# Attention with head mixing and a token and channel mixer on one core: the sums' 1e-9, the places of weight conversion, the places of v and k loads

## The chip, the cores and the metric

The kernel runs on one core of a Trainium2 chip. The metric is the device time of one launch in microseconds (us); lower is better. The engines in the text are PE (TensorE; PEld is its weight load), DVE (VectorE), ACT (ScalarE), POOL (GpSimd) and SP (SyncE), which issues nearly all DMAs.

## What is computed

```python
scores = scale * (q @ k.T)                           # 4 batches, 12 heads, 448 x 448, head_dim 64
scores = einsum('bhij,hg->bgij', scores, w_pre)      # mix the 12 heads
scores = scores - max(scores, -1)
attn = exp(scores) / (sum(exp(scores), -1) + 1e-09)
attn = einsum('bhij,hg->bgij', attn, w_post)         # mix the heads again
x = concat_heads(attn @ v)                           # (4, 448, 768)
u = x + (relu(x.T @ w_tok1) @ w_tok2).T              # 448 -> 256 -> 448
out = u + relu(u @ w_ch1) @ w_ch2                    # 768 -> 1536 -> 768
```

Everything is float32; the weights of the last two lines arrive as 64-bit numbers and are converted on the chip.

## The kernel before, in words

**Attention, tiled.** Each batch's 448 query rows are cut into four tiles T of 120, 120, 120 and 88 rows, 16 tiles in all. For a tile, `qk` (L129) makes the scores of a pair of heads on PE and copies them to the tile `s` (ACT, L146). `regroup` (L156) takes ten query rows with their 12 heads each and moves them by DMA from `s` to one of eight tiles `r`, so that 120 partitions hold (head, row) pairs. On such a group `pre` (L161) mixes heads on PE, `mx` (L171) takes the negated row maximum on DVE into the small tile `sm`, `ex` (L177) does the exponential on ACT, whose accumulator writes the row sums to `sm`, and `rec` (L188) makes the reciprocals on DVE (an add of 1e-9 at L192, the reciprocal at L193) and lets POOL scale the tile `e` with them (L195 short, L198 long). `post` (L200) mixes heads again on PE, `turn` (L213) transposes on DVE (L220), and `av` (L224) multiplies by v on PE; ACT copies one half of its result to `x` (L249), DVE adds the other (L251), and a DMA stores it (L252). Two groups sit side by side on 128 partitions and are one entry of `steps`: 92 entries, one in 23 with a single group.

**The loop.** The main loop (L447) runs J from -2 to 45, two entries of `steps` per J, in an order written out by hand that every engine follows in its own queue. In step J, `pa` and `pb` are posted and turned (entries 2J and 2J+1), `ea` and `eb` get their exponentials and `rec` (2J+2, 2J+3), `na` and `nb` their `pre` and `mx` (2J+4, 2J+5), and entries 2J+8 and 2J+9 are regrouped; what is regrouped in step J is read by `pre` in step J+2. Between these stand one `av` (`value[J]`) and mostly two `qk` (`score[J]`; three in J = 5, 6, 8, 28, 29 and 31, one beside two `av` in 10 and 33, none from 40 on). PE's order in a step is post, post, pre, av, qk, pre, qk; DVE's is turn, rec, turn, rec, mx, add of av, mx.

**PSUM.** Post, av and qk results share two buffers of a pair of banks (`pair("w", ...)`), in turn: the second qk of a step can start only when DVE's add (L251) has emptied av's buffer. `pre` has two of its own.

**Loads.** `loads[J]` are issued at the head of step J on SP's queue, before the step's regroups: q by `uses[T] - 2`; v of batch b in four parts of 384 KB, two at a time (L439); k of batch b in three parts of two DMAs of 224 KB, one part per step (L442).

**Weight conversion.** `cv_tick` (L394) works on a pipeline over `units`. One tick at position i issues the load of unit i+5 (SP, L349), copies unit i's rounded half (ACT, L370), does three bit operations of unit i+1 (DVE, L379, L383, L389), subtracts for unit i's low half (POOL, L387), clamps for unit i+2 (POOL, L361) and takes magnitudes for unit i+3 (ACT, L355). Positions start at -5; units 0 to 3 are w_tok1, 4 to 7 are w_tok2, the rest channel weights. Ticks stand in the last four steps of the loop (L476), after the loop (L580), and in the token phase (two in each `tok1`, three in each `tok2` but the first).

**After the loop** the last tile's three `av` alternate with the PE transpositions `tr` of batch 0 (L499), then `tok1` and `tok2` run for four batches, with `tr` of the next batch between them, and then the channel phase, `ch1` and `ch2`.

Of the kernel before, what the change touches and what calls it, by code (L numbers as in the profile page):

```python
# [8 lines left out]
F32 = mybir.dt.float32  # L9
# [5 lines left out]
ALU = mybir.AluOpType  # L15
AX = mybir.AxisListType
# [9 lines left out]
HP = H // 2  # L26
NR = 8
NE = 4
KD = DM // 128
NC = DC // 128  # L30
WARM = 11
# [4 lines left out]
def attn_mixer_kernel(  # L36
# [12 lines left out]
    nc = tc.nc  # L49
# [24 lines left out]
    mid = en("mid", bufs=2)  # L74
# [5 lines left out]
    kpost = mid.tile([128, 64], F32, bufs=1, name="kpost")  # L80
    et = [mid.tile([128, 2, 512], F32, bufs=1, name=f"e{i}") for i in range(NE)]
    rt = [mid.tile([128, S], F32, bufs=1, name=f"r{i}") for i in range(NR)]
    AT, V = {}, {}

    K = {}
    Q = {}
    S_t, R, E, SM, PP, PO = {}, {}, {}, {}, {}, {}
    ne = [0]

    groups = []  # L90
    first = []
# [78 lines left out]

    def mx(st):  # L171
        m = 64 * len(st)
        s = mid.tile([128, 8], F32, tag="sm", bufs=6, name="sm")
        nc.vector.tensor_reduce(out=s[:m, 0:2], in_=PP[st[0]][:m, :, :S], axis=AX.X, op=ALU.max, negate=True)  # L174
        SM[st[0]] = s

    def ex(st, x):  # L177
        m = 64 * len(st)
        s, p = SM[st[0]], PP[st[0]]
        if x == 0:  # L180
            E[st[0]] = et[ne[0] % NE]
            ne[0] += 1
        nc.scalar.activation(  # L183
            out=E[st[0]][:m, x, :S], in_=p[:m, x, :S], func=ACTF.Exp, bias=s[:m, x:x + 1], scale=1.0,
            accum_out=s[:m, 2 + x:3 + x],
        )

    def rec(st):  # L188
        m = 64 * len(st)
        s, e = SM.pop(st[0]), E[st[0]]  # L190
        PP.pop(st[0])
        nc.vector.tensor_scalar_add(out=s[:m, 4:6], in0=s[:m, 2:4], scalar1=1e-9)  # L192
        nc.vector.reciprocal(out=s[:m, 6:8], in_=s[:m, 4:6])  # L193
        w = s[:m, 6:8].unsqueeze(2)
        nc.gpsimd.tensor_tensor(  # L195
            out=e[:m, :, S:], in0=e[:m, :, 384:S], in1=w.to_broadcast([m, 2, 512 - S]), op=ALU.mult,
        )
        nc.gpsimd.tensor_tensor(out=e[:m, :, :S], in0=e[:m, :, :S], in1=w.to_broadcast([m, 2, S]), op=ALU.mult)  # L198
# [25 lines left out]
    def av(T, hp):  # L224
        b, t = divmod(T, 4)
        i0, n = IT[t]
        w = 12 if t < 3 else 9
        at_ = AT[T].rearrange("p c (g x f) -> p g c x f", g=2, x=2)
        p = pair("w", "av")
        for u in range(2):  # L230
            for j in range(JT):
                for r in range(2) if j < 3 else (u,):
                    k = slice(64 * r, 64 * r + 64)
                    for s in range(2):
                        h = 2 * hp + s
                        f = 32 * j + 5 * h
                        nc.tensor.matmul(  # L237
                            out=p[64 * s:64 * s + 64, r, 10 * w * u:10 * w * (u + 1)], lhsT=V[b][k, 6 * u + h, j, :],
                            rhs=at_[k, u, :w, :, f:f + 5], start=j == 0, stop=j == (3 if r == u else 2),
                        )  # L240
        x = late.tile([128, 2, 120], F32, tag="x", bufs=4, name="x")
        m = n // GR * GR
        y = p[:, :, :20 * w].rearrange("p r (u y) -> p r u y", u=2)
        cols = [(x[:, :, :m].rearrange("p u (k c) -> p u c k", k=GR), slice(0, m), GR)]
        if m < n:
            cols.append((x[:, :, m:n].unsqueeze(2), slice(m + 1, n + 1), n - m))
        cols = [(o, [y[:, r, :, c].rearrange("p u (c k) -> p u c k", k=k) for r in range(2)]) for o, c, k in cols]
        for o, (y0, _) in cols:
            nc.scalar.copy(out=o, in_=y0)  # L249
        for o, (_, y1) in cols:  # L250
            nc.vector.tensor_tensor(out=o, in0=y1, in1=o, op=ALU.add)  # L251
        nc.sync.dma_start(out=x_dr[b][:, hp:hp + 4:3, i0:i0 + n], in_=x[:, :, :n])  # L252

    two = (nc.sync, nc.scalar)
    one = (nc.sync, nc.sync)
# [2 lines left out]
        load_k(0, part, two)  # L258
    for i in range(2):
        nc.gpsimd.memset(kcat[i], 0.0)  # L260
    nc.gpsimd.dma_start(out=kcat[0][4:124], in_=wcat)
    for s in range(2):
        nc.gpsimd.dma_start(out=kcat[1][64 * s:64 * s + 60], in_=wcat[60 * s:60 * s + 60])
# [6 lines left out]
    for i in range(WARM):  # L270
        p = pair("w", "pw")
# [3 lines left out]
    for x in range(2):  # L275
        ps_ = slice(64 * x, 64 * x + 64)
        nc.vector.tensor_tensor(
            out=kpre[ps_, :60].rearrange("p (i g) -> p i g", i=5),
            in0=kcat[0][ps_, :12].unsqueeze(1).to_broadcast([64, 5, H]),
# [4 lines left out]
    for s in range(2):  # L284
        ps_ = slice(64 * s, 64 * s + 64)
        for hf in range(2):
            nc.gpsimd.tensor_tensor(
                out=kpost[ps_, 32 * hf:32 * hf + 30].rearrange("p (g i) -> p g i", g=6),
                in0=kcat[1][ps_, 12 + 6 * hf:18 + 6 * hf].unsqueeze(2).to_broadcast([64, 6, 5]),
# [104 lines left out]
    def cv_tick(k, eng=nc.gpsimd):  # L394
        for _ in range(k):
            i = cv_pos[0]
            if i >= cv_lim[0]:
                return
            if i + 5 < len(units):
                cv_load(i + 5)  # L400
            cv_step(i, eng)
            if 0 <= i + 2 < len(units):
                cv_clamp(i + 2)
            if 0 <= i + 3 < len(units):
                cv_abs(i + 3)
            cv_pos[0] += 1

    NS = len(steps)
    ND = NS // 2
    sf = [next(i for i, st in enumerate(steps) if st[0] == f) for f in first[:-1]] + [NS]  # L410
    loads = {J: [] for J in range(-2, ND)}
    score = {J: [] for J in range(-2, ND)}
    value = {J: [] for J in range(-2, ND)}
    for T in range(NT - 1):
        J = sf[T + 1] // 2
# [8 lines left out]
    for T in range(2, NT):  # L424
        hi = (sf[T] - 8) // 2
        lo = max((sf[T - 1] - 9) // 2 + 1, hi - 2)
        for h in range(HP):
            J = min(range(lo, hi + 1), key=lambda J: (len(score[J]) + len(value[J]), J))
            score[J].append((T, h))
    uses = {}  # L430
# [5 lines left out]
        loads[max(-2, uses[T] - 2)].append((load_q, T, one))  # L436
    for b in range(B):
        for part in range(JT):
            loads[max(0, sf[4 * b + 1] // 2 - 6) + part // 2].append((load_v, b, part))  # L439
        if b:  # L440
            for part in range(3):
                loads[uses[4 * b] - 5 + part].append((load_k, b, part, one))  # L442

    def step(i):
        return steps[i] if 0 <= i < NS else []
# [1 line left out]
    for J in range(-2, ND):  # L447
        pa, pb, ea, eb, na, nb = [step(2 * J + i) for i in range(6)]
        if J == ND - 4:
            close("early")  # L450
            open_prep()
        if J == ND - 1:
            close("ps")
            a2 = en("a2", bufs=2, side="right")
            pst = en("pst", bufs=4, space=PSUM, side="right")
        for fn, *a in loads[J]:
            fn(*a)
        if J in (ND - 3, ND - 2):
            load_x(J - ND + 3)
        for st in (pa, pb):  # L460
            if st:
                post(st)
        if ea:
            ex(ea, 1)
        if pa:
            turn(pa)
        if ea:
            rec(ea)
            ex(eb, 0)
            ex(eb, 1)  # L470
        if pb:
            turn(pb)
        if eb:
            rec(eb)
        if J >= ND - 4:
            cv_tick((2, 2, 3, 3)[J - ND])  # L476
        if na:
            pre(na)
            mx(na)
        for a in value[J][:1]:  # L480
            av(*a)
        for a in score[J][:1]:
            qk(*a)
        if nb:
            pre(nb)
            ex(na, 0)
        for a in value[J][1:]:
            av(*a)
        for a in score[J][1:]:
            qk(*a)  # L490
        if nb:
            mx(nb)
        for st in (step(2 * J + 8), step(2 * J + 9)):
            for G in st:
                regroup(G)
# [3 lines left out]
    def tr(b, hfs=(0, 1)):  # L499
        x = XR[b]  # L500
        xn = XN.get(b) or [a2.tile([128, JT - i, DM], F32R, tag=f"xn{i}", bufs=1, name=f"xn{i}") for i in range(2)]
        for hf in hfs:
            for j in range(JT):
                p = pst.tile([128, 512], F32, tag="tr", name="tr")
                for d in range(3):
                    nc.tensor.transpose(
                        out=p[:, 128 * d:128 * d + 128], in_=x[hf][:, d, min(128 * j, 320):min(128 * j, 320) + 128],
                        identity=prep["ident"],
                    )
                cs = slice(384 * hf, 384 * hf + 384)  # L510
                nc.scalar.copy(out=xn[0][:, j, cs], in_=p[:, :384])
                lo_t, r = (xn[1][:, j, cs], 0) if j < 3 else (xn[0][:64, 3, cs], 64)
                nc.vector.tensor_tensor(out=lo_t, in0=p[r:, :384], in1=f32(xn[0])[r:, j, cs], op=ALU.subtract)
        XN[b] = xn
# [27 lines left out]
    def tok2(b):  # L542
        h1 = H1.pop(b)
        x = XR.pop(b)
        us = []
        for d in range(KD):
            p = psa.tile([128, 512], F32, tag="t", bufs=4, name="pt2")
# [26 lines left out]

    av(NT - 1, 0)
    tr(0, (0,))
    av(NT - 1, 1)
    tr(0, (1,))
    av(NT - 1, 2)
    cv_tick(3)  # L580
    close("mid", "late", "atp", "ps_w")
    psa = en("psa", bufs=2, space=PSUM)
    prep["w"] = en("wres", bufs=1)
# [101 lines left out]
```

## Time and profile before

| | |
|---|---|
| median of 3 runs | 835.23 us (834.58 to 839.51) |
| the profiled execution's own time | 835.09 us |
| its span, first to last instruction | 833.0 us |
| busy in the span | PE 768.2, PEld 579.8, DVE 509.6, ACT 335.7, POOL 307.0 us |
| attention loop / its end and the token phase / channel phase | to about 377 / to about 480 / to 833 us |

How to read the rows below: times are us from the span's start. A timeline row gives start, duration, engine, line, operation, output<-input tiles, sizes and count; the square bracket says how long the engine had been idle just before, and which instruction ended that idle time. PEclk is the granted TensorE clock as a share of full speed. In the chain of work that ended last, each row is a piece of the path, followed back from the last instruction. A PE matmul's end is modelled, so that matmuls which follow each other appear to overlap.

### The profile page before, as it was taken

The numbers are of one execution on the slowest core, as the hardware profiler recorded it, in microseconds if no ns is written. First come the engines' busy times: TensorE is split into PE (matmuls) and PEld (weight loads), VectorE is DVE, ScalarE is ACT, GpSimd is POOL, SyncE is SP. The second block draws the span as 40 slices with busy tenths as digits, with TensorE's granted clock in tenths as the row PEclk, the third lists the DMA queues.
The fourth block names the chain that finished last, engine by engine and source line by source line (L and its number), as shares of the span: only waits on it lengthen the run. The fifth ranks groups of instructions, "written<-read, shape, count | busy, mean of one in ns | idle before, by whom it ended". The sixth has DMA issues, their size and how long they took to land.

```text
span 833.0 us, 21918 instructions
## 1 busy us (share of the span) xinstructions
PE 768.2 (92%) x9211; PEld 579.8 (70%) x9211; DVE 509.6 (61%) x816; ACT 335.7 (40%) x757; POOL 307.0 (37%) x292
## 2 busy tenths in 40 slices
PE   7788888999888888886899999999999999999998
PEld 3344545455445454445688899999999999999997
DVE  4867788888887788898889989964000400030002
ACT  3646656666666656554454334432000200020000
POOL 3645454555554555576536857730000000000000
PEclk9989999999999999997999999999999999999999
DMA  6874646456644643365356755543000300010001
GB/s 169 246 203 119 181 160 206 154 130 232 191 159 131 201 148 126 123 195 179 104 171 227 225 173 172 171 170 134 1 1 1 133 1 1 1 67 1 0 1 67
DMA packets 62594, 105.66 MB, mean 127 GB/s; under 512 B 20979, under 2 KB 49184, under 8 KB 61984
## 3 DMA queue, kind: packets, MB, share of 16 engines
q1 hardware_dynamic: 62080, 103.35, 39.5%
q8 instruction: 73, 1.20, 0.6%
q10 hardware_dynamic: 320, 0.87, 0.4%
q14 instruction: 25, 0.20, 0.1%
q0 software_dynamic: 96, 0.03, 0.0%
HBM read 49.18 MB, written 16.52 MB: 79 GB/s over the span
## 4 chain that ended last, share of the span: by engine, by line
PE 72%; DVE 17%; issue 4%; DMA 3%; ACT 3%; POOL 1%; SPq 0%; DVEq 0%; POOLq 0%; ACTq 0%
PE post L207 7%; PE pc L522 7%; PE pc L521 7%; PE pc L523 7%; PE po L522 7%; PE po L521 7%; PE po L523 7%; PE qk L139 7%; DVE at L220 6%; PE av L237 5%; DVE sm L192 4%; PE pre L167 3%; DVE x L251 3%; PE pt L521 2%; PE pt L522 2%
## 5 line engine op out<-in xcount | busy, mean ns | idle before, releaser
L518 DVE SCALAR_TENSOR_TENSOR rl<-pc,rh 128x448 fp32r<-128x448 f32 x48 | 29.9, 622 | 224.8 <-ACT rh L517 224.8
L198 POOL TENSOR_TENSOR e<-e,sm 128x896 f32<-128x896 f32 (+1 forms) x92 | 154.6, 1680 | 7.2
L220 DVE STREAM_TRANSPOSE at<-post 128x1024 f32<-128x1024 f32 (+1 forms) x92 | 111.9, 1216 | 49.7 <-PE post L207 49.7
L517 ACT ACTIVATE rh<-pc 128x448 fp32r<-128x448 f32 x48 | 26.0, 541 | 242.8 <-PE pc L523 242.8
L183 ACT ACTIVATE e<-pre,sm 128x448 f32<-128x448 f32 (+1 forms) x184 | 114.9, 633 | 16.0 <-DVE sm L174 15.5
L207 PE MATMUL post<-e,kpost 64*32 64x256 f32 x2880 | 100.2, 382 | 22.7 <-DVE x L251 7.5
L139 PE MATMUL qk<-k,q 64*64 64x448 f32 (+2 forms) x768 | 94.7, 546 | 24.9 <-DVE x L251 23.4
L207 PEld LDWEIGHTS post<-e,kpost 64*32 64x32 f32 x2880 | 49.6, 106 | 82.4 <-POOL e L198 33.4
L523 PE MATMUL pc<-u,w 128*128 128x448 f32 x288 | 105.2, 365 | 0.0
L522 PE MATMUL po<-rl,w 128*128 128x448 f32 x288 | 105.2, 365 | 0.0
L522 PE MATMUL pc<-u,w 128*128 128x448 f32 x288 | 105.2, 365 | 0.0
L521 PE MATMUL po<-rh,w 128*128 128x448 f32 x288 | 105.2, 365 | 0.0
L521 PE MATMUL pc<-u,w 128*128 128x448 f32 x288 | 105.2, 365 | 0.0
L523 PE MATMUL po<-rh,w 128*128 128x448 f32 x288 | 105.2, 365 | 0.0
L174 DVE TENSOR_REDUCE sm<-pre 128x2 f32<-128x896 f32 (+1 forms) x92 | 99.6, 1085 | 7.0 <-PE pre L167 6.7
L167 PE MATMUL pre<-r,kpre 64*64 64x448 f32 (+1 forms) x720 | 96.5, 553 | 5.3 <-DMA r<-s 3.0
L195 POOL TENSOR_TENSOR e<-e,sm 128x128 f32<-128x128 f32 (+1 forms) x92 | 36.7, 399 | 169.1 <-DVE sm L193 145.4
L361 POOL TENSOR_SCALAR cv_g<-cv_g 128x384 f32<-128x384 f32 (+2 forms) x56 | 87.0, 1555 | 23.6 <-ACT cv_g L355 23.6
L237 PEld LDWEIGHTS av<-at,v 64*64 64x64 f32 x2688 | 79.2, 137 | 22.8 <-DVE sm L192 10.8
L146 ACT COPY s<-qk 120x896 f32<-120x896 f32 (+1 forms) x84 | 75.4, 905 | 36.7 <-PE qk L139 33.4
L237 PE MATMUL av<-at,v 64*64 64x120 f32 (+1 forms) x2688 | 84.5, 269 | 1.2 <-DVE x L251 1.0
L139 PEld LDWEIGHTS qk<-k,q 64*64 64x64 f32 (+2 forms) x768 | 29.6, 128 | 59.9 <-DVE x L251 33.6
(71 smaller groups left out, 1060.6 us busy)
## 6 DMA issues: line engine op xcount, KB each, us to landing
r<-s SPq DMA_DIRECT2D x176, 210.0 KB
cv_r<-in_w_ch_dram SPq DMA_DIRECT2D x48, 384.0 KB
v<-in_v_dram SPq DMA_DIRECT2D x16, 384.0 KB
xr<-x_dr SPq DMA_DIRECT2D x8, 672.0 KB
u_dr<-u SPq DMA_DIRECT2D x24, 224.0 KB
ur<-u_dr SPq DMA_DIRECT2D x4, 1344.0 KB
out_dram<-ur SPq DMA_DIRECT2D x24, 224.0 KB
k<-in_k_dram SPq DMA_DIRECT2D x21, 224.0 KB
```

What stands on the lines that cost most here:

```text
L139: nc.tensor.matmul(out=p[c:c + m, s, :S], lhsT=Q[T][r, h, c:c + m], rhs=K[b][r, h, :], start=True, stop=True)
L167: nc.tensor.matmul(out=p[64 * s:64 * s + 64, x, :S], lhsT=kpre[k], rhs=rt[a % NR][k], start=True, stop=True)
L174: nc.vector.tensor_reduce(out=s[:m, 0:2], in_=PP[st[0]][:m, :, :S], axis=AX.X, op=ALU.max, negate=True)
L183: nc.scalar.activation(out=E[st[0]][:m, x, :S], in_=p[:m, x, :S], func=ACTF.Exp, bias=s[:m, x:x + 1], scale=1.0, accum_out=s[:m, 2 + x:3 + x],
L198: nc.gpsimd.tensor_tensor(out=e[:m, :, :S], in0=e[:m, :, :S], in1=w.to_broadcast([m, 2, S]), op=ALU.mult)
L207: nc.tensor.matmul(out=p[32 * a:32 * a + 32, s, 256 * hf:256 * hf + 256], lhsT=kpost[k, 32 * hf:32 * hf + 32], rhs=ek[k, :, :, a, :], star ...
L220: nc.vector.transpose(out=AT[T][:, c:c + w].rearrange("p c f -> p (c f)"), in_=p[:, :w].rearrange("p c f -> p (c f)"))
L237: nc.tensor.matmul(out=p[64 * s:64 * s + 64, r, 10 * w * u:10 * w * (u + 1)], lhsT=V[b][k, 6 * u + h, j, :], rhs=at_[k, u, :w, :, f:f + 5] ...
L361: nc.gpsimd.tensor_scalar(out=g[:P], in0=g[:P], scalar1=MAG_MIN, scalar2=MAG_MAX, op0=ALU.max, op1=ALU.min,)
L521: nc.tensor.matmul(out=p, lhsT=a[0], rhs=x[0], start=first, stop=False)
L522: nc.tensor.matmul(out=p, lhsT=a[0], rhs=x[1], start=False, stop=False)
L523: nc.tensor.matmul(out=p, lhsT=a[1], rhs=x[0], start=False, stop=last)
```

## The change

The tile `sm`, so far drawn from a pool of six buffers of 8 columns, becomes six persistent tiles of 10 columns, filled with 1e-9 once at the start. ACT's accumulator writes the two row sums to columns 2 and 4, so that each has a 1e-9 beside it in columns 3 and 5. DVE's add of a constant (L192) becomes a sum over pairs of columns. Conversion ticks in the last four steps go from 2, 2, 3, 3 to 2, 1, 1, 3; after the loop one comes behind each of the two `tr`, and three become two at the end. Parts of v are loaded in four steps, one each, the last one step before the first use; k's three parts are loaded two in one step and one in the next, nearer to the first use.

```diff
+NM = 6
+    smt = [mid.tile([128, 10], F32, bufs=1, name=f"sm{i}") for i in range(NM)]
     def mx(st):
-        s = mid.tile([128, 8], F32, tag="sm", bufs=6, name="sm")
+        s = smt[ns[0] % NM]
+        ns[0] += 1
     def ex(st, x):
-            accum_out=s[:m, 2 + x:3 + x],
+            accum_out=s[:m, 2 + 2 * x:3 + 2 * x],
     def rec(st):
-        nc.vector.tensor_scalar_add(out=s[:m, 4:6], in0=s[:m, 2:4], scalar1=1e-9)
-        nc.vector.reciprocal(out=s[:m, 6:8], in_=s[:m, 4:6])
+        nc.vector.tensor_reduce(
+            out=s[:m, 8:10], in_=s[:m, 2:6].rearrange("p (x y) -> p x y", y=2), axis=AX.X, op=ALU.add
+        )
+        nc.vector.reciprocal(out=s[:m, 6:8], in_=s[:m, 8:10])
@@ start
+    for m in smt:
+        nc.vector.memset(m, 1e-9)
@@ loads
-            loads[max(0, sf[4 * b + 1] // 2 - 6) + part // 2].append((load_v, b, part))
+            loads[sf[4 * b + 1] // 2 - 4 + part].append((load_v, b, part))
-                loads[uses[4 * b] - 5 + part].append((load_k, b, part, one))
+                loads[uses[4 * b] - 3 + part // 2].append((load_k, b, part, one))
@@ main loop
-            cv_tick((2, 2, 3, 3)[J - ND])
+            cv_tick((2, 1, 1, 3)[J - ND])
@@ after the loop
     tr(0, (0,))
+    cv_tick(1)
     av(NT - 1, 1)
     tr(0, (1,))
+    cv_tick(1)
     av(NT - 1, 2)
-    cv_tick(3)
+    cv_tick(2)
```

By the two formulas, the steps of the loads are:

| | v parts 0 to 3, before | after | k parts 0 to 2, before | after |
|---|---|---|---|---|
| batch 0 | 0, 0, 1, 1 | -1, 0, 1, 2 | at the start | at the start |
| batch 1 | 8, 8, 9, 9 | 10, 11, 12, 13 | 0, 1, 2 | 2, 2, 3 |
| batch 2 | 20, 20, 21, 21 | 22, 23, 24, 25 | 12, 13, 14 | 14, 14, 15 |
| batch 3 | 31, 31, 32, 32 | 33, 34, 35, 36 | 23, 24, 25 | 25, 25, 26 |

## Rows read from the trace of the kernel before

**Rows 1.** The page, chain that ended last, shares by engine

```profile
PE 72%; DVE 17%; issue 4%; DMA 3%; ACT 3%; POOL 1%; SPq 0%; DVEq 0%; POOLq 0%; ACTq 0%
```

**Rows 2.** Windows: stretch, length, PE, PEld, DVE, ACT, POOL busy, PEclk, DMA share, GB/s

```profile
50.00:58.00 8.00, 7.65 (x88) 5.06 (x88) 1.79 (x3) 1.53 (x3) 1.92 (x2) 0.60 0.72 201
58.00:340.00 282.00, 252.36 (x5479) 138.40 (x5476) 226.37 (x328) 177.89 (x408) 145.81 (x143) 1.00 0.53 164
...
384.00:388.00 4.00, 3.89 (x56) 2.71 (x58) 2.94 (x6) 0.27 (x2) 2.01 (x3) 0.50 0.32 91
...
411.70:414.00 2.30, 2.30 (x11) 2.30 (x12) 2.20 (x5) 1.08 (x3) 0.00 (x0) 0.50 0.00 0
```

**Rows 3.** Instructions on the tile sm: DVE's reduce and add, ns min/median/max, first and last start

```profile
L174 DVE TENSOR_REDUCE sm<-pre x92: 1070/1086/1107, 18.8 to 371.4; 128x2 f32<-128x896 f32 x88, 64x2 f32<-64x896 f32 x4
L192 DVE TENSOR_SCALAR sm<-sm x92: 116/170/1287, 21.7 to 374.9; 128x2 f32<-128x2 f32 x88, 64x2 f32<-64x2 f32 x4
```

**Rows 4.** Timeline of one step, J = 17, up to the next step's second qk

```profile
166.86 1.68 POOL L198 TENSOR_TENSOR e<-e,sm 128x896 f32<-128x896 f32 x1
167.28 1.28 DVE L192 TENSOR_SCALAR sm<-sm 128x2 f32<-128x2 f32 x1
...
168.33 0.58 ACT L249 COPY x<-av 128x240 f32<-128x240 f32 x1 [1.92 <-PE av L237]
...
168.69 1.09 DVE L174 TENSOR_REDUCE sm<-pre 128x2 f32<-128x896 f32 x1
168.78 1.00 PE L167 MATMUL pre<-r,kpre 64*64 64x448 f32 x8
...
169.69 0.56 DVE L251 TENSOR_TENSOR x<-av,x 128x240 f32<-128x240 f32 x1
...
170.31 0.98 PE L139 MATMUL qk<-k,q 64*64 64x448 f32 x8 [0.53 <-DVE x L251]
...
178.01 0.98 PE L139 MATMUL qk<-k,q 64*64 64x448 f32 x8 [0.51 <-DVE x L251]
```

**Rows 5.** PE's waits from 58 to 345 us; PE in J = 6; L192 in J = 22 and 23

```profile
PE qk L139 <- DVE x L251: 23.4, 33, 1.3
...
81.80 1.73 PE L139 MATMUL qk<-k,q 64*64 64x448 f32 x16 [0.86 <-DVE x L251]
...
204.41 0.13 DVE L192 TENSOR_SCALAR sm<-sm 128x2 f32<-128x2 f32 x1
...
205.27 0.13 DVE L192 TENSOR_SCALAR sm<-sm 128x2 f32<-128x2 f32 x1
...
211.38 0.12 DVE L192 TENSOR_SCALAR sm<-sm 128x2 f32<-128x2 f32 x1
```

**Rows 6.** SP's queue and PE in J = 1 to 3, and the chain between them

```profile
38.58 2.13 SPq L107 DMA_DIRECT2D k<-in_k_dram  x2
...
40.82 9.39 DMA r<-s
...
50.35 1.95 PE L167 MATMUL pre<-r,kpre 64*64 64x448 f32 x5 [3.01 <-DMA r<-s]
```

**Rows 7.** PE's second post in J = 41 and 42 (steps without qk)

```profile
352.99 1.10 PE L207 MATMUL post<-e,kpost 64*32 64x256 f32 x32 [1.10 <-POOL e L198]
...
359.43 1.10 PE L207 MATMUL post<-e,kpost 64*32 64x256 f32 x32 [1.07 <-POOL e L198]
```

**Rows 8.** Timeline from the last two steps to the first tok1

```profile
382.49 0.56 ACT L249 COPY x<-av 128x240 f32<-128x240 f32 x1
...
383.39 0.57 DVE L251 TENSOR_TENSOR x<-av,x 128x240 f32<-128x240 f32 x1
...
384.11 1.93 PE L207 MATMUL post<-e,kpost 64*32 64x256 f32 x16 [6.75 <-DVE x L251]
...
396.70 0.44 PE L521 MATMUL pt<-xn,t 128*128 128x384 f32 x1
```

**Rows 9.** PE at the second half of batch 1's transpositions

```profile
411.66 2.82 PE L506 MATMUL tr<-ident,xr 128*128 128x128 f32 x12 [4.15 <-DVE xn L513]
```

More of the change, by code (lines that the diff above doesn't have):

```diff
@@ L87, in attn_mixer_kernel @@
     S_t, R, E, SM, PP, PO = {}, {}, {}, {}, {}, {}
-    ne = [0]
+    ne, ns = [0], [0]
     groups = []
```

## The prediction

> **What bounds the kernel now.** I read the chain that ended last first: PE carries 72% of it and DVE 17% [rows 1]. Windows then say where the 17% can lie. From 58 to 340 us PE is busy for 252.4 of 282.0 us at full clock, so about 30 us of the loop are PE's gaps, and no other engine is near full there (DVE 226.4, ACT 177.9, POOL 145.8) [rows 2]. So neither PE's work alone nor DVE's sum is the limit: something late each time is. The instructions on the tile `sm`, by line, show a misfit: L192, an add on 128x2 numbers, takes 170 ns in the median, yet up to 1287 [rows 3]. The timeline of one step explains it: the second L192 starts at 167.28 and ends at 168.56, POOL's long L198 runs from 166.86 to 168.54 [rows 4]. The add ends when POOL's operation ends. I found this in 45 of the 92, once per step, and in the 40 from J = 4 on it takes 1.26 to 1.29 us; where the second add starts before L198 it takes 0.13, as in J = 22 [rows 5].
>
> What that delays, in the same step: behind the add on DVE stand the reciprocal, `mx` (168.69), then L251 (169.69 to 170.25), which empties av's bank pair, and the second qk starts right behind it at 170.31, after 0.53 us of idle PE [rows 4]. PE's waits give the total: qk waited 23.4 us for L251 in 33 cases [rows 5]. That is most of the 30 us. Three further losses stand outside this pattern: a wait for a regroup in J = 3 [rows 6], one of 6.75 us at the end of the loop [rows 8], one of 4.15 us in the token phase [rows 9]; around each the clock is down at 0.5 [rows 2].
>
> **The change part by part.** The sum goes by the profiled execution, 835.09 us, which lies 0.14 below the median.
>
> *The add becomes a reduce.* One instruction replaces one. A reduce of four numbers isn't in the trace. From below: the shortest L192, 0.12 us [rows 3]. From above: it waits as L192 does, 1.28 us. L174 is a reduce: 1.085 us for 896 numbers, 1.2 ns each, and 1.07 to 1.11 us in every instance, though many run beside L198 (the one at 168.69 ends beside the L198 that follows it) [rows 3, 4]. It reads PSUM, so it isn't quite the same; still it is the nearest row by operation, and I take the reduce as never waiting, 0.15 us.
>
> On this the Trainium skill has a rule (SBUF — State Buffer, Who interferes with whom): DVE and GpSimd share one pair of ports, a tensor_scalar between SBUF tiles can take the pair and then fully blocks behind a GpSimd operation, while tensor_reduce on this chip never contends. The first half agrees with L192's ends in rows 4; the second half no run here shows yet. By the rule the sum is the one below; without it, with L192 as the model, it is the second rival.
>
> Now a step again, with J = 17's rows: add and reciprocal end at 167.6 instead of 168.7. `mx` runs to 168.69 (its `pre` ended before). ACT's copy ends at 168.91, so L251 now waits for ACT and runs 168.96 to 169.53. The second qk could start at 169.58. PE, which issues the next matmul about 0.75 us after `pre`'s start at 168.78, is ready at 169.53. So the step shrinks by 170.31 - 169.58 = 0.73 us and no more: what is late next is PE itself and ACT's copy, both within 0.05 us. The period falls from 7.70 [rows 4] to 6.97. J = 22, where the add didn't wait, is a natural trial: its period is 211.38 - 204.41 = 6.97 [rows 5], though its second post is half as long. In the six steps that follow one with three qk, PE idles 0.86 us rather than 0.53 (J = 6 [rows 5]), and the same working gives 1.0. For J = 4 to 39 without 22: 27 x 0.73 + 6 x 1.0 + 2 x 0.7 (the two with two av) = 27.1 us. The idle time in the trace alone is 23.4; the rest is that modelled ends overlap. I take 26.8, range 19 to 27.1.
>
> J = 40 to 43 have no qk. There the second post waits 1.1 us for POOL's L198 [rows 7]: POOL's second scaling can't start until the late reciprocal. At least the 0.4 us between the two scalings goes; at most all 1.15 us, since DVE is full there. The loop post, turn, rec, two scalings, post comes to 11.2 us for two steps, so 5.6 instead of 6.45: 4 x 0.8 = 3.2 us, range 1.5 to 4.6.
>
> J = -1 to 2: the add waits there as well (0.87 to 1.26 us), but DMA is the near limit: 2 us, range 0 to 2.8.
>
> The other edits of this part cost nothing: six fills of 10 columns on DVE, about 0.1 us each like the other small fills there, lie before 3 us, while PE's first real matmul waits for k until 7.67. A persistent tile comes round every six entries like the pool's buffer did, so no wait is added.
>
> *v and k.* J = 3 starts its `pre` 3.01 us late, for regroups issued in J = 1 at 40.82 that landed 9.39 us later; then PE ran at clock 0.6 in the mean from 50 to 58 [rows 2, 6]. J = 3 took 14.05 us, against 7.70. Before that regroup SP had issued four v parts and two k parts, 4 x 384 + 4 x 224 = 2432 KB; with the change it is three v parts, 1152 KB. At 201 GB/s [rows 2] the 1280 KB fewer are 6.4 us, more than the 3.0 us of wait plus what the earlier steps run ahead. J = 3 should take 7.0 us: 7.1 saved, of which I take 6, range 0.7 to 7.1. The moved DMAs are the same 16 of v and 18 of k, about 0.6 us of SP's queue each. They now stand ahead of other regroups: J = 2, 14 and 25 issue four k DMAs at their heads (J = 2 and 25 a v part too), 2.4 to 3 us of SP time and up to 1280 KB, 6.4 us at that rate. These steps' regroups are read two steps on, 14 us later at the new pace, so I cost them at nothing; if that cover fails, a step pays what J = 3 paid, 7.1 us.
>
> *Ticks.* In J = 44 three ticks stood in DVE's and ACT's queues ahead of av's copy and add. The copy ran at 382.49, though av had ended at 375.5, and the last post waited 6.75 us [rows 8], after which PE ran at 0.50 [rows 2]. Now J = 44 has one tick, which has nothing for DVE (the pipeline is two positions younger: only a load, a clamp on POOL and a magnitude on ACT). The post then waits for POOL's scaling alone, near 378.0. The three ticks of J = 45 bring the first nine DVE operations ahead of the next L251: DVE took 7 us for such nine, from 376.34 to L251 at 383.39 [rows 8], so from about 379.8 the second av of the last tile can start near 386, with 2.6 us of idle PE, and `tok1` near 390.5 instead of 396.70 [rows 8]. That is 6.2. An idle of 3.0 us halved the clock before [rows 6, 2], so 2.6 may; I take 5.5, range 2 to 8. w_tok1's last unit gets its low half near 391.6; `tok1` asks for it 1.6 us after its start, so this just fits.
>
> In the token phase PE waited 4.15 us at 411.66 [rows 9] behind DVE, which itself stood behind clamps and subtractions on POOL, 1.0 to 1.8 us each: five ticks' worth from 397.6 to 410.8. Now four ticks do their share there, half of it on 224 columns, some 8 us of POOL work begun 6 us earlier. The wait goes, and with it the 2.3 us at clock 0.50 [rows 2] that count for about half: 4.0, range 0 to 5.5. The ticks left over are 13 - 11 = 2 units: they slide through later ticks of the token phase, where one spare existed, and one tick remains before the channel phase, whose first weights are by then long done: nothing.
>
> **Sum.** 26.8 + 3.2 + 2 + 6 + 5.5 + 4 = 47.5 us. 835.1 - 47.5 = 787.6, told as 788 us.
>
> **The rivals.**
>
> 1. *The tail gives nothing back.* For: w_tok1's last unit has no slack, and a second wait of 3 us halves the clock. Against: the 6.75 us have a plain cause that leaves. Without the 9.5 us: 797.
> 2. *The reduce waits as the add did.* For: both read and write SBUF beside L198. Against: L174. Only loads and ticks are left: 6 + 5.5 + 4 = 15.5, so 819.6.
> 3. *Regroups come late* behind the bunched k parts, once per batch: for, the 9.39 us of rows 6; against, DMA's share of 0.53 in the loop. Three stalls of 7.1 us: 809.
> 4. *Slower.* The same mechanism in many steps: with shorter steps the lead of two steps falls from 15.4 to 14 us, and v and k are now issued in 20 steps. From seven stalls of 7.1 us on nothing is left of the 47.5; eight give 844. Against: in rows 6 even 9.39 us came at a DMA load that the change halves.
>
> **How the numbers follow.** Forecast 0.70, rival 1 0.15, rival 3 0.08, rival 2 0.05, rival 4 0.02. All lower ends of the ranges with the forecast's mechanism leave 19 + 1.5 + 0 + 0.7 + 2 + 0 = 23 us (812), all upper ends 27.1 + 4.6 + 2.8 + 7.1 + 8 + 5.5 = 55 us (780). The range of 776 to 808 holds the forecast and rival 1, cuts the far end where all terms fail together, and leaves 4 us below for a step shorter than PE's modelled ends suggest. A change of 1% (8.4 us) is about what a measurement here tells from none. Only rival 4, and rival 2 with another loss, come near or above that line: faster 0.96, within 1% 0.02, slower 0.02.
>
> **What would show it.** In the profile after: L192's successor at 0.13 to 0.17 us in all 92, also while L198 runs; first recs of neighbouring steps 6.9 to 7.1 us apart; PE's wait of qk for L251 under 5 us in the loop; no regroup wait in J = 3 and a clock of 1.00 around 45 to 55 us; PE's last post of the loop waiting about 1.5 us or less. Wrong would be: reduces of over 1 us, steps that stay at 7.7 with another releaser (ACT's copy, a regroup), or a new wait of 5 us or more at `tok1`.

## The result, and the profile after

The changed kernel takes 798.34 us (797.7 to 798.9), the kernel before 836.97 beside it: a ratio of 0.9538, 95% interval 0.9503 to 0.9573. That is 38.6 us less; 47.5 had been forecast, and 798 lies inside the range. The profiled execution took 798.18 us, with a span of 796.1. Of run 12's six times in the table further down, one (804.16 us) fell in the chip's slower state; its median counts that time, its ratio does not.

The page after, busy time by engine and the chain that ended last (compare [rows 1]):

```profile
PE 765.5 (96%) x9211; PEld 578.4 (73%) x9211; DVE 462.3 (58%) x822; ACT 334.1 (42%) x757; POOL 305.3 (38%) x292
...
PE 82%; DMA 7%; DVE 3%; ACT 2%; POOL 2%; issue 2%; SPq 1%; DVEq 0%; POOLq 0%; ACTq 0%
```

DVE's share of the chain fell from 17% to 3%, and its busy time by 47 us: what had counted as work was waiting. PE's work is the same within 3 us. DMA, 3% before, is 7% now, a first hint at the missing part of the forecast. The instructions on `sm` (compare [rows 3]):

```profile
L177 DVE TENSOR_REDUCE sm<-pre x92: 1061/1082/1093, 18.5 to 343.0; 128x2 f32<-128x896 f32 x88, 64x2 f32<-64x896 f32 x4
L195 DVE TENSOR_REDUCE sm<-sm x92: 103/115/158, 21.3 to 346.9; 128x2 f32<-128x4 f32 x88, 64x2 f32<-64x4 f32 x4
```

All 92 pair sums take 0.10 to 0.16 us. The step J = 17 again, in the order of [rows 4]:

```profile
157.25 1.68 POOL L203 TENSOR_TENSOR e<-e,sm 128x896 f32<-128x896 f32 x1
157.67 0.11 DVE L195 TENSOR_REDUCE sm<-sm 128x2 f32<-128x4 f32 x1
...
157.97 1.07 DVE L177 TENSOR_REDUCE sm<-pre 128x2 f32<-128x896 f32 x1
...
158.66 0.58 ACT L254 COPY x<-av 128x240 f32<-128x240 f32 x1 [1.92 <-PE av L242]
159.10 1.00 PE L169 MATMUL pre<-r,kpre 64*64 64x448 f32 x8
159.28 0.59 DVE L256 TENSOR_TENSOR x<-av,x 128x240 f32<-128x240 f32 x1 [0.23 <-ACT x L254]
...
159.92 0.19 PEld L141 LDWEIGHTS qk<-k,q 64*64 64x64 f32 x8 [0.59 <-DVE x L256]
159.92 0.98 PE L141 MATMUL qk<-k,q 64*64 64x448 f32 x8
...
166.91 0.98 PE L141 MATMUL qk<-k,q 64*64 64x448 f32 x8
```

The sum runs inside POOL's long scaling and takes no notice of it. So it is throughout: 45 of the 92 pair sums start while a long scaling runs, and none takes over 0.16 us, whereas the 45 adds that started so in the kernel before all ended 0.02 to 0.03 us behind the scaling. DVE's add of av (L256) now waits for ACT's copy, 0.23 us. The second qk follows PE's `pre` without idle time of PE, though its weights (PEld) are still loaded only when L256 has ended. The period is 166.91 - 159.92 = 6.99 us. From 58 to 340 us PE is busy for 272.6 us instead of 252.4 [rows 2]:

```profile
58.00:340.00 282.00, 272.61 (x5970) 153.80 (x5974) 209.12 (x360) 187.79 (x438) 158.46 (x158) 0.99 0.59 178
```

At the start it went otherwise. SP's queue, the chain and PE in J = 2 to 4 (compare [rows 6], J = 1 to 3 there):

```profile
42.50 3.33 SPq L109 DMA_DIRECT2D k<-in_k_dram  x4
47.14 5.42 SPq L161 DMA_DIRECT2D r<-s  x4
...
48.90 9.71 DMA r<-s
...
56.88 1.06 PE L169 MATMUL pre<-r,kpre 64*64 64x448 f32 x2 [2.74 <-DMA r<-s]
58.66 1.02 PE L169 MATMUL pre<-r,kpre 64*64 64x448 f32 x3 [0.71 <-DMA r<-s]
...
58.00:62.00 4.00, 3.34 (x46) 2.74 (x50) 1.09 (x1) 0.00 (x0) 1.06 (x1) 0.50 0.71 219
```

The wait for regroups did not go; it moved from J = 3, where 0.34 us of it is left, to J = 4. The last row is the window behind it: the clock is at 0.50, its lower level, as it was behind the wait in J = 3 before. By the reciprocals of the two traces, J = 5 starts at 68.67 us; before, it started at 68.66. All that J = -1 to 3 had gained was lost in J = 4, which took 14.22 us.

The tail, PE's waits and the first `tok1` (compare [rows 8, 9]):

```profile
350.01 1.07 PE L212 MATMUL post<-e,kpost 64*32 64x256 f32 x16 [1.00 <-POOL e L203]
...
357.95 2.44 PE L242 MATMUL av<-at,v 64*64 64x90 f32 x56 [2.52 <-DVE x L256]
...
363.61 0.44 PE L528 MATMUL pt<-xn,t 128*128 128x384 f32 x1
...
375.72 2.07 PE L513 MATMUL tr<-ident,xr 128*128 128x128 f32 x12 [1.17 <-DVE xn L520]
```

The last post waits 1.00 us instead of 6.75, the transpositions 1.17 instead of 4.15, and a wait of 2.52 us has come before av, about as worked out (2.6).

### The profile page after: what moved, and what is told of

The parts are those of the page before. It is cut to its first block, busy times and chain, and to the rows that moved or that the text cites. A ratio compares the mean times of both kernels' runs of the same rounds, so it can differ in the third digit from the quotient of the medians.

```text
span 796.1 us, 21930 instructions
## 1 busy us (share of the span) xinstructions
PE 765.5 (96%) x9211; PEld 578.4 (73%) x9211; DVE 462.3 (58%) x822; ACT 334.1 (42%) x757; POOL 305.3 (38%) x292
## 4 chain that ended last, share of the span: by engine, by line
PE 82%; DMA 7%; DVE 3%; ACT 2%; POOL 2%; issue 2%; SPq 1%; DVEq 0%; POOLq 0%; ACTq 0%
PE post L212 9%; PE pre L169 8%; PE av L242 7%; PE pc L528 7%; PE pc L529 7%; PE pc L530 7%; PE po L528 7%; PE po L530 7%; PE po L529 7%; PE qk L141 7%; DMA r<-s 4%; PE pt L528 2%; PE pt L530 2%; PE pt L529 2%; POOL e L203 1%
## 5 line engine op out<-in xcount | busy, mean ns | idle before, releaser
L525 DVE SCALAR_TENSOR_TENSOR rl<-pc,rh 128x448 fp32r<-128x448 f32 x48 | 29.8, 621 | 218.1 <-ACT rh L524 218.1
L524 ACT ACTIVATE rh<-pc 128x448 fp32r<-128x448 f32 x48 | 26.1, 543 | 232.4 <-PE pc L530 232.3
L169 PE MATMUL pre<-r,kpre 64*64 64x448 f32 (+1 forms) x720 | 101.1, 554 | 7.5 <-DMA r<-s 4.4
L212 PEld LDWEIGHTS post<-e,kpost 64*32 64x32 f32 x2880 | 49.5, 106 | 70.8 <-issue 38.6
L141 PE MATMUL qk<-k,q 64*64 64x448 f32 (+2 forms) x768 | 97.7, 547 | 1.1 <-DMA k<-in_k_dram 0.5
L368 POOL TENSOR_SCALAR cv_g<-cv_g 128x384 f32<-128x384 f32 (+2 forms) x56 | 87.1, 1558 | 18.3 <-ACT cv_g L362 18.3
L200 POOL TENSOR_TENSOR e<-e,sm 128x128 f32<-128x128 f32 (+1 forms) x92 | 36.9, 401 | 143.2 <-ACT e L186 86.6
L148 ACT COPY s<-qk 120x896 f32<-120x896 f32 (+1 forms) x84 | 75.5, 907 | 17.4 <-PE qk L141 11.1
L169 PEld LDWEIGHTS pre<-r,kpre 64*64 64x64 f32 (+1 forms) x720 | 33.3, 133 | 44.2 <-issue 31.9
```

The lines of the kernel that those rows point to most:

```text
L141: nc.tensor.matmul(out=p[c:c + m, s, :S], lhsT=Q[T][r, h, c:c + m], rhs=K[b][r, h, :], start=True, stop=True)
L169: nc.tensor.matmul(out=p[64 * s:64 * s + 64, x, :S], lhsT=kpre[k], rhs=rt[a % NR][k], start=True, stop=True)
L212: nc.tensor.matmul(out=p[32 * a:32 * a + 32, s, 256 * hf:256 * hf + 256], lhsT=kpost[k, 32 * hf:32 * hf + 32], rhs=ek[k, :, :, a, :], star ...
L368: nc.gpsimd.tensor_scalar(out=g[:P], in0=g[:P], scalar1=MAG_MIN, scalar2=MAG_MAX, op0=ALU.max, op1=ALU.min,)
```

## The experiments

Each ratio is to runs of the kernel before on the same chip, where its median lay between 836.9 and 840.4 us.

| run | median, us | ratio, 95% interval |
|---|---|---|
| changed kernel | 798.34 | 0.9538 (0.9503 to 0.9573) |
| 1 add of a constant put back | 828.17 | 0.9897 (0.9834 to 0.9961) |
| 2 pair sum alone | 811.02 | 0.9685 (0.9635 to 0.9735) |
| 3 ticks alone | 827.95 | 0.9884 (0.9834 to 0.9933) |
| 4 loads alone | 833.85 | 0.9953 (0.9917 to 0.9989) |
| 5 changed, old loads | 800.20 | 0.9550 (0.9510 to 0.9591) |
| 6 changed, k of batch 1 later | 798.59 | 0.9526 (0.9481 to 0.9572) |
| 7 pair sum by two-tensor add | 827.96 | 0.9890 (0.9860 to 0.9920) |
| 8 as 6, weight loads early | 798.39 | 0.9529 (0.9485 to 0.9572) |
| 9 one part per step | 798.70 | 0.9535 (0.9492 to 0.9578) |
| 10 k of batch 1 latest | 796.00 | 0.9505 (0.9461 to 0.9548) |
| 11 no k of batch 1 | 793.15 | 0.9472 (0.9444 to 0.9500) |
| 12 k of batch 1 at the start | 793.24 | 0.9429 (0.9392 to 0.9466) |

**1. The add of a constant put back.**

```diff
-        nc.vector.tensor_reduce(out=s[:m, 8:10], in_=s[:m, 2:6]..., axis=AX.X, op=ALU.add)
+        nc.vector.tensor_scalar_add(out=s[:m, 8:10], in0=s[:m, 2:4], scalar1=1e-9)
...
-            accum_out=s[:m, 2 + 2 * x:3 + 2 * x],
+            accum_out=s[:m, 2 + x:3 + x],
```

> The changed kernel with the add of a constant in place of the pair sum (accumulator columns 2 and 3 again, the tiles persistent as after the change). Theory (the add waits for POOL's long scaling, and that is the loop's gain): the second add of a step takes 1.28 us again, steps go back from 7.0 to 7.7 us, and the time is 798 + 28 = 826 us (823 to 830). Rival (the gain comes from loads and ticks, or from persistent tiles): 798 to 805 us.

Measured: 828.17 us, 29.8 more. The add on `sm` and POOL's scaling in its trace:

```profile
L195 DVE TENSOR_SCALAR sm<-sm x92: 117/170/1290, 21.7 to 376.8; 128x2 f32<-128x2 f32 x88, 64x2 f32<-64x2 f32 x4
...
166.03 1.68 POOL L201 TENSOR_TENSOR e<-e,sm 128x896 f32<-128x896 f32 x1
166.45 1.28 DVE L195 TENSOR_SCALAR sm<-sm 128x2 f32<-128x2 f32 x1
```

The add ends at 167.73, the scaling at 167.71; steps take 7.8 us. The persistent tiles have no part in it, for they are there in this run too. The theory holds.

**7. The pair sum by an add of two tensors.** It asks which property of the instruction lets it pass, and it is the Trainium skill's rule (SBUF — State Buffer, Who interferes with whom) put to the test: a second input from SBUF is to make DVE wait too, behind a GpSimd operation that reads SBUF.

```diff
-        nc.vector.tensor_reduce(out=s[:m, 8:10], in_=s[:m, 2:6]..., axis=AX.X, op=ALU.add)
+        nc.vector.tensor_tensor(out=s[:m, 8:10], in0=s[:m, 2:6:2], in1=s[:m, 3:6:2], op=ALU.add)
```

> The changed kernel with the pair sum as an add of two tensors, the sums and the 1e-9 columns, instead of a reduce. Theory by the rule on the shared ports (a DVE instruction with two SBUF inputs is blocked by a POOL instruction that reads SBUF): the second add of a step takes near 1.28 us again and the time is 825 to 828 us. Rival (only the add of a constant, with its doubled rate, is blocked): 0.12 to 0.2 us each and 798 us.

Measured: 827.96 us. Its add beside POOL's scaling:

```profile
L195 DVE TENSOR_TENSOR sm<-sm x92: 110/162/1280, 21.8 to 376.8; 128x2 f32<-128x2 f32 x88, 64x2 f32<-64x2 f32 x4
...
166.41 1.68 POOL L201 TENSOR_TENSOR e<-e,sm 128x896 f32<-128x896 f32 x1
166.83 1.27 DVE L195 TENSOR_TENSOR sm<-sm 128x2 f32<-128x2 f32 x1
```

The same numbers from the same columns, and the whole gain of the pair sum is gone. The trace agrees with the Trainium skill's rule: the add of a constant and the add of two tensors wait to within 0.03 us of the scaling's end, the reduce never waits.

**2 to 4. Each part alone, on the kernel before.** The edits are the three parts of the diff shown with the change.

> The kernel before with the pair sum and the persistent tiles alone. Theory: the loop from J = 5 on gains 26 us and its last steps 2, while the regroup wait in J = 3 stays and swallows what earlier steps gain: 836 - 28 = 808 us (805 to 811). Rival (the parts need each other: with the old loads the shorter steps wait for regroups more often): 815 us or more.

Measured: 811.02 us, 25.9 less than before. J = 3 waits 4.70 us for regroups and takes 15.16 us; J = 33, where the old loads issue two v parts a step earlier, takes 10.35 us instead of 9.00. Nearer to the theory (808) than to the rival, though the rival's effect is there.

> The kernel before with the moved ticks alone. Theory: the last post's wait of 6.75 us and most of the 4.15 us wait in the token phase go: 836 - 9 = 827 us (825 to 829). Rival (the tail's gain needs the shorter last steps that the pair sum gives): 831 to 836 us.

Measured: 827.95 us, 9.0 less. The tail's gain needs nothing else.

> The kernel before with the new places of the v and k loads alone. Theory (the stall of about 7 us moves from J = 3 to J = 4, behind the v part and four k DMAs that J = 2 now issues ahead of its regroups): 836 us, within 2; J = 3 takes under 9 us and J = 4 about 14. Rival (as predicted: the stall goes, and it came back in J = 4 only because the shorter steps of the changed kernel outrun the DMAs): 829 to 831 us.

Measured: 833.85 us, 3.1 less, between the two. J = 3 takes 7.70 us and J = 4 9.86, not 14: with the slow steps of the kernel before PE waits there for regroups no more than 0.55 us at a time and the clock stays at 1.00 (50 to 66 us). The three parts alone give 25.9 + 9.0 + 3.1 = 38.0 us; together they give 38.6.

**5. The changed kernel with the old loads.**

```diff
-            loads[sf[4 * b + 1] // 2 - 4 + part].append((load_v, b, part))
+            loads[max(0, sf[4 * b + 1] // 2 - 6) + part // 2].append((load_v, b, part))
...
-                loads[uses[4 * b] - 3 + part // 2].append((load_k, b, part, one))
+                loads[uses[4 * b] - 5 + part].append((load_k, b, part, one))
```

> The changed kernel with the old places of the v and k loads. Theory (the early stall only changes its step, but with shorter steps the old pairs of v parts also make a regroup late near J = 33): 801 to 803 us, J = 3 near 15 us and J = 33 near 10. Rival (the new places are worth nothing beside the pair sum): 798 us. Rival of the prediction (they are worth 6 us or more): 804 us or more.

Measured: 800.20 us; its interval overlaps that of the changed kernel, so between shorter steps the new places are worth 2 us or nothing. J = 3 takes 13.99 us, J = 33 8.80.

**6 and 8. k of batch 1 one step later, then the weight loads early as well.**

```diff
-                loads[uses[4 * b] - 3 + part // 2].append((load_k, b, part, one))
+                J = uses[4 * b] - 3 + part // 2
+                if b == 1:
+                    J = uses[4] - (1, 1, 2)[part]
+                loads[J].append((load_k, b, part, one))
...
-        if part == 0:
+        if b not in K:
             K[b] = early.tile([128, HP, S], F32, tag="k", bufs=2, name="k")
```

> The changed kernel with k of batch 1 issued one step later (its part 2, which is used first, in J = 3, parts 0 and 1 in J = 4). Theory (J = 4 takes 14.2 us because J = 2 issues four k DMAs ahead of its regroups): J = 4 takes 7 to 8 us, J = 5 starts near 61.5 instead of 68.7, and the time is 791 us (790 to 794). Rival (DMA has a fixed backlog after the start, so the stall moves on to J = 5 or 6): 797 to 799 us.

Measured: 798.59 us. J = 4 takes 7.00 us and J = 5 starts at 60.44, as the theory said; but then J = 5 and 6 take 10.58 and 10.40, so the rival wins. J = 5's third qk belongs to a new tile, and ACT's copy into `s` waits until the regroups that read this buffer have landed; they stand behind the moved k. PE waits 3.10 us there, and the clock falls again, to 0.60 from 70.2 to 74.5 us:

```profile
69.20 0.91 ACT L148 COPY s<-qk 120x896 f32<-120x896 f32 x1 [3.29 <-DMA r<-s]
...
70.25 1.32 PE L212 MATMUL post<-e,kpost 64*32 64x256 f32 x32 [3.10 <-ACT s L148]
```

Run 8 adds this:

```diff
             open_prep()
+            for i in range(5):
+                cv_load(i)
...
-            if i + 5 < len(units):
+            if 0 <= i and i + 5 < len(units):
```

> As the run with k of batch 1 later, and the first five loads of token weights issued together in J = 42 instead of one per tick. Theory (in J = 45 ACT's magnitudes wait for weight loads, in front of av's copy, which leaves PE idle for 2.5 us): the wait falls under 1 us, 1 to 3 us less than that run. Rival (DVE's nine operations alone fill that time): the same time as that run within 1 us.

Measured: 798.39 us, and PE's wait before av is still 2.52 us. ACT's magnitudes, which waited 1.06 and 0.25 us for weight loads there in the changed kernel, wait for none here, so this theory falls. The nine DVE operations ahead of L256, with 0.95 us of waiting for POOL's clamp among them, fill the time up to its start at 358.8.

**9 and 10. Other orders.** The tile of k is drawn as in run 6, here and in run 12. Run 9 spreads v of batch 0 over J = -2 to 1 and k of batch 1 over 2 to 4; run 10 puts k in 3 to 5.

```diff
-                loads[uses[4 * b] - 3 + part // 2].append((load_k, b, part, one))
+                J = uses[4 * b] - 3 + part // 2
+                if b == 1:
+                    J = (3, 4, 2)[part]      # run 10: (4, 5, 3)
+                loads[J].append((load_k, b, part, one))
...
-            loads[sf[4 * b + 1] // 2 - 4 + part].append((load_v, b, part))
+            loads[sf[4 * b + 1] // 2 - 4 + part - (b == 0)].append((load_v, b, part))      # run 9 only
```

> The changed kernel with never more than one part of v or k per step at the start: v of batch 0 in J = -2 to 1, k of batch 1 in J = 2 (part 2), 3 (part 0) and 4 (part 1). Theory (until about 65 us the bytes that all loads and regroups need set the pace, whatever their order): J = 7 still starts between 81 and 86 us and the time is 796 to 799 us. Rival (it is the bunch ahead of a regroup that costs): J = 7 starts near 78 and the time is 791 to 793 us.

> The changed kernel with k of batch 1 in J = 3 (part 2), 4 (part 0) and 5 (part 1), the latest places that its uses allow, v as in the change. Theory (bytes set the pace): 796 to 799 us, with the wait in J = 5 or 6. Rival (the bunch costs): 791 to 793 us.

Measured: 798.70 and 796.00 us; J = 7 starts at 82.49 and 81.36. Order changes which step pays, and at most 2.3 us of the sum, less than the intervals can tell.

**11. Fewer bytes.** Batch 1 uses k of batch 0, whose tile is there anyway, so this run leaves out three parts, 1344 KB, and its scores for that batch are not the right ones.

> The changed kernel without the loads of k of batch 1; batch 1 uses batch 0's k in its place, so its output differs, and 1344 KB less are moved before 60 us. Theory (bytes set the pace there, some 210 GB/s): 6.4 us are saved, J = 7 starts near 78 instead of 84.7, and the time is 792 us (791 to 794). Rival (DMA latency or SP's queue, not bytes): J = 7 starts after 82 and the time is 796 us or more.

Measured: 793.15 us, and J = 7 starts at 76.15; J = 4, 5 and 6 take 6.98, 8.18 and 7.84 us, as long as a step with two or three qk takes later. So it is the loads of k that cost the time. Whether by their bytes, this run can't tell alone, for six DMAs of about 0.6 us each on SP's queue go with them. SP's own waits suggest that the transfers and not the issuing held things up: by the profile, SP waited 9.6 us for DMAs between 20 and 60 us in the changed kernel and 2.0 us here. A run with fewer issues and the same bytes is missing.

**12. The same bytes where DMA has room.** Before 20 us there was some; the windows of the kernel before:

```profile
8.00:12.00 4.00, 4.00 (x48) 2.49 (x41) 2.24 (x4) 2.31 (x5) 0.43 (x2) 1.00 0.76 163
12.00:20.00 8.00, 6.70 (x64) 3.05 (x55) 5.09 (x8) 3.45 (x8) 0.00 (x0) 1.00 0.39 146
```

```diff
     load_q(1, one)
+    for part in (2, 0):
+        load_k(1, part, one)
...
-                loads[uses[4 * b] - 3 + part // 2].append((load_k, b, part, one))
+                J = uses[4 * b] - 3 + part // 2
+                if b == 1:
+                    if part != 1:
+                        continue
+                    J = 4
+                loads[J].append((load_k, b, part, one))
```

> The changed kernel with two of batch 1's three k parts (2 and 0, 896 KB) issued at the very start, behind q of tile 1, where SP is idle from 5 to 13 us and DMA's share falls to 0.39, and part 1 in J = 4; v as in the change. Theory (from 20 to 60 us the bytes to be moved set the pace, and 896 KB less at 210 GB/s are 4.3 us): J = 7 starts near 80 us instead of 84.7, and the time is 794 us (792 to 796), less than both kernels. Rival (the early k delays the first regroups by as much as it saves later): J = 0 starts 2 us or more later than 28.7, and the time is 797 us or more.

Measured: 793.24 us, ratio 0.9429 (0.9392 to 0.9466), whose interval lies below the changed kernel's. The same windows of this run (the share, reckoned from packets' times, can pass 1.00), then the first reciprocal of J = 7 in it and, in the fence after it, in the changed kernel:

```profile
8.00:12.00 4.00, 4.00 (x45) 3.08 (x46) 2.16 (x4) 2.23 (x5) 0.44 (x2) 1.00 1.03 236
12.00:20.00 8.00, 6.71 (x61) 3.35 (x56) 5.18 (x8) 3.46 (x7) 0.00 (x0) 1.00 0.68 213
...
76.57 0.17 DVE L198 RECIPROCAL sm<-sm 128x2 f32<-128x2 f32 x1
```

```profile
84.72 0.17 DVE L198 RECIPROCAL sm<-sm 128x2 f32<-128x2 f32 x1
```

The idle DMA time of the first 20 us takes the k, PE does the same work there (6.71 us against 6.70), J = 0 starts at 27.33, no later, and J = 7 starts 8.2 us earlier. The median is 5.1 us lower; the ratios lie further apart because the kernel before took 840.39 us on that chip. J = 7 had been expected near 80, from 4.3 us of bytes at 210 GB/s; the profile shows nearly twice that, and 6.3 us of it are left at J = 44. The bytes at that rate don't account for all of it. This version is faster than the kernel before and, by the ratios, than the changed kernel; those two were not timed side by side.

## Why the prediction was right, and where it was not

**The add (32 us with its share of early steps and the last ones).** Right in mechanism and size where the loop is steady. From the start of J = 5 to that of J = 40 the two profiles differ by 279.2 - 253.1 = 26.1 us (26.8 forecast for J = 4 to 39). J = 17 has 6.99 us (6.97), limited by ACT's copy and PE's order, as worked out. J = 40 to 43 gave 2.2 instead of 3.2: the second post still waits for POOL in every second step, and steps of 6.3 and 5.5 us take turns where 5.6 had been forecast for all. Run 1 takes the reduce away and the gain with it; run 7 shows that being a sum isn't what counts. Choosing L174, the nearest row by operation, over L192, the row of the instruction replaced, was the right choice between the ends.

**The ticks (9.5 us).** Right: 9.0 in run 3. In the profiles the stretch from J = 44 to `tok1` shrank by 23.0 - 18.3 = 4.7 us (5.5 forecast), that from `tok1` to the first `tok2` matmul by 17.4 - 13.9 = 3.5 (4.0). The two units that slid on cost nothing: from the first `tok2` matmul to the end it is 418.9 us before and 418.6 after.

**v and k, and the early steps (6 + 2 us).** Wrong, and this is 8 of the 10.6 us missing between the profiles (their spans differ by 36.9 us, against 47.5 forecast): J = 5 starts no earlier than before. The step that failed is the sentence "These steps' regroups are read two steps on, 14 us later at the new pace, so I cost them at nothing". In J = 2 the regroups were issued from 47.14 on, behind the 3.33 us of four k DMAs and 1.2 us in which SP waited, by the profile, for an earlier regroup to land; `pre` of J = 4 was due at 54.14. That is a lead of 7 us, not 14, for a regroup is issued at the end of its step and read at the head of the step after next. [rows 6] had shown it: issued from 40.82, due at 50.35 - 3.01 = 47.34, 6.5 us later. In the steady loop of the changed kernel, too, it is 9.5 us (issued from 160.54 in J = 17, read from 170.05). The regroup that was waited for landed at 58.61, 9.71 us after its issue. The price given for that case, "a step pays what J = 3 paid", 7.1 us, is what J = 4 paid: 14.22 us against 6.97 in run 12.

Behind this lies a wrong question. I counted the bytes ahead of one regroup, and the bytes taken away from there had only been put ahead of the next. In all twelve profiles where the whole k of batch 1 moves after 20 us (before, changed, runs 1 to 10) the first reciprocal of J = 7 comes between 81.4 and 87.8 us, whatever the order and the steps' length. Runs 1, 4 and 7 say little here: their steps are slow, and PE waits for regroups only 0.4 to 1.0 us in all from 20 to 85 us, against 4.4 in the changed kernel. Runs 6 and 8, with one order of loads, differ by 4.5 us, so nothing finer is to be read from one execution. Only with fewer bytes in that stretch (run 11) or some of them moved ahead of 20 us (run 12) does it start at 76.2 and 76.6. The window from 20 to 60 us fits this, here in the kernel before, then in the changed one:

```profile
20.00:60.00 40.00, 31.01 (x518) 14.82 (x520) 29.99 (x43) 22.26 (x56) 20.91 (x21) 0.91 0.81 225
```

```profile
20.00:60.00 40.00, 32.85 (x543) 14.51 (x543) 27.51 (x48) 23.38 (x58) 24.84 (x25) 0.97 0.81 215
```

DMA runs at a share of 0.81 in both, against 0.53 and 0.59 from 58 to 340 us. That is no proof, for run 12 has 0.80 there and PE waits for no regroup in it. That the loads of k in this stretch cost the time is shown by runs 11 and 12; that they do so by their bytes and not by their number is argued. Run 4 got 3 us from the loads since its steps are slow enough to be fed; this and the two terms of 2 and 6 us were not additive, as my sum took them to be.

**The rivals.** The second (the reduce waits) is refuted by the rows of L195. The first (nothing from the tail) is refuted by run 3; that its 797 us came so near the measured 798 is a coincidence, for the 9.5 us of the tail came in large part and the 8 us of the early steps did not. The fourth (slower) did not come. The third came true in one of its three places, J = 4; behind J = 14 and 25, with the same four k DMAs, steps 15, 16 and 26 take 7.0 us and J = 27 7.43. Not settled: single steps that are long in one execution and not in another (J = 35 took 11.31 us in run 6, 6.95 in the changed kernel; J = 27, the rival's third place, 9.58 in run 10 and 6.99 in run 12, with the same loads there).

## What to carry to other kernels

If an instruction of a few elements has two durations, compare its end with the other engines' ends before anything else: it may be waiting inside its own busy time, and another instruction for the same numbers may not wait. When loads fill a stretch, as at the start here, their order may only choose the step that pays; look for a stretch where the queues are idle, and move bytes there. A gain in steps that precede such a stretch is not to be added to one behind it. And a transfer's lead is read in the timeline, from its issue to its use, not from a count of steps.

## What was not expected of the hardware

An add over two columns of SBUF tiles waited as long as the add of a constant (1.27 against 1.28 us), while a reduce over the same four numbers took 0.115 us in the median beside the same POOL operation. And after PE's idle times of 2.74 and 0.71 us with little work between them the granted clock, 1.00 from 50 to 54 us, was 0.50 from 58 to 62; after one of 2.52 us at the end of the loop, which began at 355.4, it was 0.69 in the mean from 356 to 361, against 1.00 from 350 to 355:

```profile
356.00:361.00 5.00, 3.05 (x59) 2.85 (x60) 4.78 (x12) 3.32 (x12) 2.99 (x4) 0.69 0.37 105
```
